# A causal-attention and two-MLP kernel on one Trainium2 core: a new order for the start of the attention, scores issued in two steps, and nine chunks of the third matrix prepared early

## The chip, the core and the metric

The kernel runs on one NeuronCore of a Trainium2 chip. Its engines take their instructions in order and independently of each other: TensorE (PE in the profile; its weight loads are PEld), VectorE (DVE), ScalarE (ACT), GpSimd (POOL), and SyncE (SP), which here only issues DMAs. The metric is the device time of one execution in microseconds (us).

## What is computed

```python
def _attn_ref(q, k, v):                       # each 2 x 12 x 448 x 64
    scores = np.matmul(q, k.transpose(0, 1, 3, 2)) / np.sqrt(64)
    scores = np.where(np.triu(np.ones((448, 448), bool), k=1), -1e9, scores)
    attn = np.exp(scores - np.max(scores, axis=-1, keepdims=True))
    attn = attn / (np.sum(attn, axis=-1, keepdims=True) + 1e-09)
    return np.matmul(attn, v)

def _moe_ref(x, w_in, w_out):                 # x: 896 x 768, w_in: 768 x 2048, w_out: 2048 x 768
    h = x @ w_in
    return (h * np.clip(h + 3.0, 0.0, 6.0) / 6.0) @ w_out

def _moe2_ref(x, w_in, w_out, a, b):          # the same sizes
    h = x @ w_in
    P = a[0] + a[1] * h + a[2] * h**2 + a[3] * h**3
    Q = 1.0 + np.abs(b[0]) * np.abs(h) + np.abs(b[1]) * h**2
    return (P / (Q + 1e-06)) @ w_out
```

The attention's result, with the heads side by side, is the `x` of the first MLP, and its result is that of the second. Weights come as float64.

## The kernel before

The 24 attention matrices (2 batches, 12 heads) are worked as 12 **pairs** n0 to n11: a pair is two heads of one batch (n = 2 hp + batch). In a pair the 448 rows of the scores are 7 blocks r of 64 rows, block r being 64(r+1) columns wide (causal). For each pair:

- **scores** (L458): 32 recorded matmuls on quarters of the array (64x64), all seven blocks at once, into four PSUM banks;
- **max** (L472, DVE), **exp** with its row sum (L479, ACT), both block by block; then for two groups of blocks, (6, 5, 0) and (4, 3, 2, 1): **bias** (L491, adds 1e-9 to the sums, POOL), **reciprocal** (L495, DVE) and **norm** (L501 on ACT, L503 on DVE and POOL);
- **transpose** (L511, two groups of 14 matmuls, array in two row halves, 64x128), and four **moves** (L346 on DVE, L344 on ACT) of the transposed blocks `et` out of PSUM;
- **apply** (L533, 36 recorded matmuls with V, array in two column halves, 128x64);
- **x hi** and **x rest** (L541 and L545): the result is split into a rounded part and a remainder, both fp32r.

The loads of q and k (`qk_load`, L414) and of V (`v_load`, seven DMAs per head pair) are issued on SP, but for two of the first pair's.

The four weight matrices (numbered 0 to 3) are cut in 128x128 tiles and stored three to a **chunk**: chunks 0 to 31 are matrix 0, 32 to 63 matrix 1, and from 64 on tiles of matrices 2 and 3 alternate. A chunk is loaded as 64-bit numbers (raw, five buffers), its top bits are taken on ACT (**top**, L662), joined on DVE (**join**, L667), rounded to fp32r (**w hi**, copied on ACT, POOL for some of the first four chunks) and its remainder taken (**w rest**, L685, DVE; POOL allowed for the first four). Some chunks of the last phase are prepared **early**, during matrices 0 and 1, written to DRAM (`kept`) and fetched back later: `early` holds the chunks c from `first` (64) up to the sixteenth from the end with c % 3 < 2. A **product** (L755) is one weight tile against both batches: six matmuls of 448 columns (hi-hi, hi-lo, lo-hi for each batch). There are 384 products, 2304 such matmuls. Products of matrix 0 may start as soon as a prepared chunk and the x of the first pairs are there; a few stand among the last pairs' attention.

What stands where is decided before the launch by a planner (class `Program`): it lists every step with the engines it may run on, an estimated cost, a time `at` and a table `DUE` of offsets per kind of step, places the steps on engines one by one, and then writes each engine's program in the planned order. At run time each engine goes through its own list in order and waits where its inputs are late.

At the start POOL fills `ident` and `mask`, and PE runs `WARM` matmuls of `ident` with itself that nobody reads (L398).

Of the kernel before, what the change touches and what calls it, by code (L numbers as in the profile page):

```python
# [20 lines left out]
CP = 64  # L21
NCH = 7
KC = 3
NA = 3
WARM = 10
SKEW = 64
LINE = 256
EARLY = 2, 3
LATE = 16
LAG = 3  # L30
MASKED = -8.0e9
# [9 lines left out]
class Program:  # L41
# [14 lines left out]
    BANKS = 8  # L56

    TILING = {"scores": "quarters", "transpose": "rows", "apply": "columns"}
    DRAIN = 0.16
    STAY = 11.93  # L60
    LOOK = {"pe": 0.302, "dve": 0.091, "act": 0.080, "pool": 0.000, "dma": 0.000}
    UNTIL = 90.0
# [5 lines left out]
    def add(self, kind, at, engines, fn, *args, reads=(), writes=(), new=()):  # L68

        self.ops.append((kind, at, engines, fn, args, tuple(reads), tuple(writes), tuple(new)))
# [150 lines left out]
def c_mm(n, passes):  # L223
# [4 lines left out]
DUE = {  # L228
    "load": 44.71,
    "keep": 0.00,  # L230
    "fetch": -20.00,
    "load v": -368.72,
    "norm": -159.02,
    "scores": 151.68,
    "max": -187.04,
    "exp": -138.64,
    "bias": -218.27,
    "reciprocal": -106.79,
    "transpose": -387.45,
    "move": 102.72,  # L240
    "apply": -96.69,
    "x hi": -163.28,
    "x rest": -28.48,
    "constants": 141.71,
    "w load": 418.94,
    "top": 318.26,
    "join": 411.50,
    "w hi": -217.67,
    "w rest": 106.68,
    "product": 0.00,  # L250
    "relu": -145.17,
    "gate": -250.64,
    "g hi": -349.62,
    "g rest": 161.82,
    "y hi": 20.80,
# [17 lines left out]
PAIR = 5.5  # L273
SHIFT = {0: -215.51, 1: -135.50, 2: -51.43, 10: 34.54, 11: 54.71}

# [19 lines left out]
def tile_attention_moe_moe2(  # L295
# [13 lines left out]
    B, D, H, S = qT.shape  # L309
# [4 lines left out]
    chunks = plan(KM, KF)  # L314
# [84 lines left out]

    add("constants", -50, {"pool": 1.5}, a_masks, writes=["masks"])  # L400
    for x in range(VB):
        add("constants", -49, {"pool": 0.4}, a_empty, x, writes=[("empty", x)])
    add(
        "constants", -49, {"pe": 0.4 * WARM}, a_warm, reads=["masks"], writes=["warm"],
        new=[("o", "warm")],
    )

    def qk_load(e, which, hp, batches):

        if (which, hp) not in tiles:  # L410
            tiles[which, hp] = at.tile([P, B, S], F32, tag=which, name=f"{which}{hp}", bufs=rings[which])
        src = (qT if which == "qr" else kT).rearrange("b d h s -> d b h s")
        for j in range(2):
            e.dma_start(tiles[which, hp][halves[j], batches], src[:, batches, 2 * hp + j])  # L414
# [10 lines left out]
    STRAIGHT, SWAPPED = (6, 5, 0), (4, 3, 2, 1)  # L425
    SCORES = 0, 2, 6, 4, 5, 1, 3
    BANKS = ((6, 0), (4, 2), (5,), (3, 1))
    GROUPS = [
# [15 lines left out]

    def a_scores(e, n, banks):
        q, k = (tiles[which, n // B][:, n % B] for which in ("qr", "kr"))
        for b, held in zip(banks, BANKS):
            col = 0
            for r in held:
                tiles["sc", n, r] = bank[b][:, col:col + (r + 1) * CP]  # L450
                col += (r + 1) * CP
        for r in SCORES:
            w = (r + 1) * CP
# [94 lines left out]

    order = 6, 0, 5, 4, 2, 3, 1
    for n in range(len(pairs)):  # L550
        t, last = PAIR * n + SHIFT.get(n, 0.0), n == len(pairs) - 1
        b, hp = pairs[n]
        for which in ("kr", "qr"):

            group, whole = (which, "all", hp), hp > 0
            if whole and b:
                continue
            add(
                "load", t, {"act" if n == 0 and which == "qr" else "dma": 1.26}, qk_load, which, hp,
                slice(0, B) if whole else slice(b, b + 1),  # L560
                writes=[(which, x) for x in range(n, n + (B if whole else 1))] + [group] * (b == 0),
                new=[(which, group)] if b == 0 else (),
            )
        if b == 0:
# [3 lines left out]
            )  # L568
        sc = [("sc", n, held) for held in BANKS]
        add(  # L570
            "scores", t, {"pe": 1.42}, a_scores, n, reads=[(w, *x) for w in ("kr", "qr") for x in ((n,), ("all", hp))],
            writes=sc + ["scored"] * last, new=[("s", key) for key in sc],
        )
        for late, r in enumerate(order):
            w, first, mine = (r + 1) * CP, late == 0, next(held for held in BANKS if r in held)
            add(
# [8 lines left out]
                writes=[("e", n, r), ("st", n, r)],  # L585
            )
        for part, held in enumerate((STRAIGHT, SWAPPED)):
            add(
                "bias", t + 2 * part, {"pool": 0.2}, a_bias, n, part,
                reads=[("st", n, r) for r in held] + [("stat", n)], writes=[("r", n, part)],  # L590
# [56 lines left out]

    add("constants", -55, {"pool": 0.7}, a_tops, writes=["tops"])

# [49 lines left out]
    def add_chunk(i, t, early=()):  # L699
# [12 lines left out]
        x = [("x", hp, b) for hp in range(KM) for b in range(B)] if early and i == early[0] else []  # L712
        act, dve = ({**e, "pool": c} if i < 4 else e for e, c in ((act, 0.5), (dve, 1.05)))
        add(
# [193 lines left out]
    first = next(c for c, what in enumerate(chunks) if what[0][0] == 2)  # L908
    early = [c for c in range(first, len(chunks) - LATE) if c % EARLY[1] < EARLY[0]]
    whole = first * KC * c_mm(S, 3 * B)  # L910
# [83 lines left out]
```

## Time and profile before

| | us |
|---|---|
| median of 3 runs (the other two 542.49 and 721.15) | 542.8 |
| the profiled execution, its own time | 541.71 |
| the profiled execution, span from first to last instruction | 539.9 |

| engine | busy us | share of the span |
|---|---|---|
| PE | 527.1 | 98% |
| DVE | 360.9 | 67% |
| ACT | 341.2 | 63% |
| POOL | 49.3 | 9% |

The mean granted TensorE clock is 0.994 of full speed (2.4 GHz); the DMA engines moved 164 GB/s on average. POOL works only in the first seventh of the span, where the attention is; after that PE runs products to the end. Matmul records overlap each other, so that a busy PE is not yet a PE at its peak: what it does in a stretch is better read from the starts of its groups of matmuls.

### The profile page before, as it was taken

What the parts mean: (1) busy time and instruction counts of PE and PEld (TensorE: products, weight loads), DVE (VectorE), ACT (ScalarE), POOL (GpSimd) and SP (SyncE); (2) the same over time, 40 slices, a digit from 0 to 9 for tenths busy, and PEclk for the clock granted to TensorE, in tenths of its full rate; (3) what the DMA queues carried; (4) which work ended last, traced back from release to release, by engine and by line L of the source; (5) the groups of instructions that cost most, each with busy time, mean ns of one, the idle gap of its engine ahead of it and who ended that gap; (6) DMA issues with size and microseconds to landing.
All of it is one profiled execution on the core that took longest, in us unless ns stands there. A gap on an engine that the chain in (4) does not pass through costs nothing.

```text
span 539.9 us, 9598 instructions
## 1 busy us (share of the span) xinstructions
PE 527.1 (98%) x3476; PEld 484.7 (90%) x3476; DVE 360.9 (67%) x801; ACT 341.2 (63%) x733; POOL 49.3 (9%) x116
## 2 busy tenths in 40 slices
PE   5899999999999999999999999999999999999997
PEld 5678879999999999999999999899999999999996
DVE  4699976677777765455443289988888888843310
ACT  4799966677777755555543299767776677645210
POOL 4598530000000000000000000000000000000000
PEclk9799999999999999999999999999999999999999
DMA  6886262487877777767774233432443244246000
GB/s 168 230 250 179 60 205 89 136 276 231 276 230 250 238 266 245 261 225 243 243 259 162 87 91 115 127 109 87 122 128 102 87 120 124 79 126 216 29 35 34
DMA packets 41583, 88.28 MB, mean 164 GB/s; under 512 B 4672, under 2 KB 16960, under 8 KB 41536
## 3 DMA queue, kind: packets, MB, share of 16 engines
q1 hardware_dynamic: 41376, 87.45, 51.7%
q8 instruction: 27, 0.44, 0.3%
q10 hardware_dynamic: 160, 0.23, 0.1%
q14 instruction: 20, 0.16, 0.1%
HBM read 72.32 MB, written 15.34 MB: 162 GB/s over the span
## 4 chain that ended last, share of the span: by engine, by line
PE 78%; DVE 6%; ACT 1%; DMA 1%; issue 1%; ACTq 0%
PE bank L755 77%; DVE p L804 1%; DVE qy L828 1%; DVE p L807 1%; DMA w<-kept 1%; DVE p L832 1%; PE bank L533 1%; DVE p L830 1%; DVE qy L820 1%; DVE rl L814 1%; DVE w L685 0%; ACT p L800 0%; ACT qy L794 0%; PE bank L511 0%; ACT top L662 0%
## 5 line engine op out<-in xcount | busy, mean ns | idle before, releaser
L685 DVE TENSOR_TENSOR w<-full,w 128x384 fp32r<-128x384 f32 x92 | 51.3, 557 | 111.4 <-ACT w L344 111.4
L755 PE MATMUL bank<-yh,w 128*128 128x448 f32 x384 | 112.7, 363 | 0.0
L662 ACT ACTIVATE top<-raw 128x384 f16<-128x384 bf16 x128 | 80.4, 639 | 49.3 <-DVE full L667 39.4
L344 ACT ACTIVATE w<-full 128x384 fp32r<-128x384 f32 x93 | 48.7, 524 | 80.6 <-PE bank L755 80.6
L755 PE MATMUL bank<-rh,w 128*128 128x448 f32 x384 | 97.2, 362 | 0.3 <-DMA w<-kept 0.3
L755 PE MATMUL bank<-xh,w 128*128 128x448 f32 x384 | 93.3, 363 | 0.0
L755 PE MATMUL bank<-ph,w 128*128 128x448 f32 x384 | 92.3, 361 | 0.0
L755 PEld LDWEIGHTS bank<-rh,w 128*128 128x128 f32 x384 | 71.8, 188 | 5.9 <-ACT qy L823 0.6
L755 PEld LDWEIGHTS bank<-yh,w 128*128 128x128 f32 x384 | 72.1, 188 | 5.3 <-DVE p L807 0.6
L755 PEld LDWEIGHTS bank<-ph,w 128*128 128x128 f32 x384 | 72.0, 187 | 4.9
L755 PEld LDWEIGHTS bank<-xh,w 128*128 128x128 f32 x384 | 71.6, 187 | 5.1
L667 DVE SCALAR_TENSOR_TENSOR full<-raw,top 128x384 uint32<-128x384 uint32 x128 | 68.9, 554 | 1.2 <-issue 0.3
L755 PE MATMUL bank<-yl,w 128*128 128x448 f32 x192 | 69.2, 361 | 0.0
L755 PE MATMUL bank<-rl,w 128*128 128x448 f32 x192 | 54.5, 362 | 0.0
L755 PE MATMUL bank<-xl,w 128*128 128x448 f32 x192 | 54.2, 363 | 0.0
L755 PE MATMUL bank<-pl,w 128*128 128x448 f32 x192 | 54.2, 363 | 0.0
L479 ACT ACTIVATE e<-e,stat 128x448 f32<-128x448 f32 (+6 forms) x84 | 41.6, 499 | 10.0 <-DVE stat L472 8.8
L755 PEld LDWEIGHTS bank<-yl,w 128*128 128x128 f32 x192 | 35.9, 187 | 2.5
L755 PEld LDWEIGHTS bank<-xl,w 128*128 128x128 f32 x192 | 36.0, 188 | 2.4
L755 PEld LDWEIGHTS bank<-pl,w 128*128 128x128 f32 x192 | 36.0, 188 | 2.3
L472 DVE CUSTOM_DVE_ANT_0 e<-bank,mask 128x256 f32<-128x256 f32 (+6 forms) x84 | 30.6, 414 | 11.2 <-PE bank L458 11.1
L755 PEld LDWEIGHTS bank<-rl,w 128*128 128x128 f32 x192 | 36.0, 187 | 2.3
(58 smaller groups left out, 633.6 us busy)
## 6 DMA issues: line engine op xcount, KB each, us to landing
raw<-in_w SPq DMA_DIRECT2D x128, 383.8 KB, 3.8
kept<-ws SPq DMA_DIRECT2D x32, 384.0 KB, 4.4
w<-kept SPq DMA_DIRECT2D x32, 384.0 KB, 3.4
out_T<-o SPq DMA_DIRECT2D x12, 224.0 KB, 2.1
kr<-in_kT SPq DMA_DIRECT2D x10, 224.0 KB, 3.8
qr<-in_qT SPq DMA_DIRECT2D x10, 224.0 KB, 4.5
v<-in_v SPq DMA_DIRECT2D x12, 128.0 KB, 3.9
v<-in_v SPq DMA_DIRECT2D x12, 96.0 KB, 3.7
```

The source lines that it names most:

```text
L344: e.activation(out, in_, AF.Copy)
L472: e.tensor_tensor_reduce(e_tile(n, r), tiles.pop(("sc", n, r)), over, -0.125, 3.0e38, ALU.add, ALU.min, tiles["stat", n][:, 0, at_:at_ + 1],)
L479: e.activation(t, t, AF.Exp, bias=stat[:, 0, at_:at_ + 1], scale=-1.0, accum_out=stat[:, 1, at_:at_ + 1],)
L533: e.matmul(o[halves[j], r * CP:(r + count) * CP], vt[:, c, halves[j]], et[slot][:, x * CP:(x + count) * CP], start=g == 0 and m == 0, stop ...
L662: e.activation(out, raw[i].bitcast(BF16)[:, :, :, 2], AF.Copy)
L667: e.scalar_tensor_tensor(full[i].bitcast(U32), bits, 13, top.pop(i), ALU.logical_shift_right, ALU.bitwise_or)
L685: e.tensor_tensor(split[i][:, 1], full.pop(i), split[i][:, 0], ALU.subtract)
L755: e.matmul(sums[which, m, b], split[i][:, w, j, :], x, start=k == 0 and n == 0, stop=last and n == 2,)
L804: e.tensor_tensor(p, p, h, ALU.mult)
L807: e.scalar_tensor_tensor(p, p, cneg[:, 1:2], h, ALU.add, ALU.mult)
L814: e.tensor_tensor(gs[3, b, m][1], p, gs[3, b, m][0], ALU.subtract)
L820: e.tensor_tensor(q, q, y, ALU.mult)
```

## The change

- `WARM`, the number of unread matmuls, goes from 10 to 6, and POOL fills `ident` and `mask` first and the two `top` buffers last instead of first.
- The first two pairs' q and k loads are single steps per half: one half of each is issued on SP and the other may be issued on ACT. The table's new numbers put the loads of the second head pair ahead of the first V.
- Scores are two steps of two banks, blocks (5, 4, 2) and (6, 3, 0, 1), instead of one of four; max and exp run over the blocks in the order 5, 6, 0, 4, 2, 3, 1 (as the table lets them), no longer 6, 0, 5, 4, 2, 3, 1.
- For pairs n0, n10 and n11 the bias is done on ACT or DVE, and no longer on POOL.
- The remainder of a weight chunk is never taken on POOL.
- The first nine chunks of the last phase (64 to 72) are all early: 35 early chunks, 32 before.
- `DUE`, `SHIFT`, `STAY`, `LOOK` have other numbers, and `HURRY` moves the later steps of the first and last pairs.

```diff
-WARM = 10
+WARM = 6
+WHOLE = 9
...
-    add("constants", -50, {"pool": 1.5}, a_masks, writes=["masks"])
+    add("constants", -60, {"pool": 1.5}, a_masks, writes=["masks"])
...
-    SCORES = 0, 2, 6, 4, 5, 1, 3
-    BANKS = ((6, 0), (4, 2), (5,), (3, 1))
+    BANKS = (((5,), (4, 2)), ((6, 0), (3, 1)))
+    SCORES = (5, 4, 2), (6, 3, 0, 1)
...
-    order = 6, 0, 5, 4, 2, 3, 1
+    order = 5, 6, 0, 4, 2, 3, 1
...
+            for parts in ((0,), (1,)) if n == 0 else ((0, 1),):
+                add(
+                    "load", t, {"act" if parts == (1,) else "dma": 0.63 * len(parts)}, qk_load, which, hp,
...
+        for step in range(2):
+            sc = [("sc", n, held) for held in BANKS[step]]
+            add(
+                "scores", t + step, {"pe": 0.71}, a_scores, n, step,
...
-                "bias", t + 2 * part, {"pool": 0.2}, a_bias, n, part,
+                "bias", t + 2 * part, {"pool": 0.2} if 0 < n < 10 else {"act": 0.2, "dve": 0.1}, a_bias, n, part,
...
-    add("constants", -55, {"pool": 0.7}, a_tops, writes=["tops"])
+    add("constants", -40, {"pool": 0.7}, a_tops, writes=["tops"])
...
-        act, dve = ({**e, "pool": c} if i < 4 else e for e, c in ((act, 0.5), (dve, 1.05)))
+        if i < 4:
+            act = {**act, "pool": 0.5}
...
-    early = [c for c in range(first, len(chunks) - LATE) if c % EARLY[1] < EARLY[0]]
+    early = [
+        c for c in range(first, len(chunks) - LATE) if c < first + WHOLE or c % EARLY[1] < EARLY[0]
+    ]
```

What this moves on the engines is seen at three places. The first is SP's list from its start; `kr0`, `qr0` are the first head pair (n0 and n1), `kr1`, `qr1` the second (n2 and n3), `v0` the first V. Before:

```order
L414 DMA kr0_107<-in_kT 64x448 x4
L414 DMA qr0_112<-in_qT 64x448 x2
L419 DMA v0_99<-in_v 64x4x128
L420 DMA v0_99<-in_v 64x3x128
L419 DMA v0_99<-in_v 64x4x128
L420 DMA v0_99<-in_v 64x3x128
L422 DMA v0_99<-in_v 64x2x128 x3
L414 DMA kr1_183<-in_kT 64x2x448 x2
L414 DMA qr1_191<-in_qT 64x2x448 x2
```

In the change (ACT's list begins with one `kr0` and one `qr0` load, where it had two of `qr0`):

```order
L417 DMA kr0_107<-in_kT 64x448
L417 DMA qr0_121<-in_qT 64x448
L417 DMA kr0_107<-in_kT 64x448 x2
L417 DMA qr0_121<-in_qT 64x448 x2
L417 DMA kr1_140<-in_kT 64x2x448 x2
L417 DMA qr1_151<-in_qT 64x2x448 x2
L422 DMA v0_99<-in_v 64x4x128
```

The four loads for n2 and n3 went ahead of the seven of V.

The second place is ACT's list in the middle of the attention; `e` rows are exps, `et` rows moves, `xh` rows x hi. Before, from the first exp of n6:

```order
L479 ACTIVATE e00_91,stat6_703<-e00_91,stat6_703 128x448
L479 ACTIVATE e00_91,stat6_703<-e00_91,stat6_703 128x64
L479 ACTIVATE e20_93,stat6_703<-e20_93,stat6_703 128x384
L479 ACTIVATE e10_92,stat6_703<-e10_92,stat6_703 128x320
L344 ACTIVATE xh1_84<-bank1_74 128x448
L479 ACTIVATE e10_92,stat6_703<-e10_92,stat6_703 128x192
L479 ACTIVATE e30_94,stat6_703<-e30_94,stat6_703 128x256
L479 ACTIVATE e30_94,stat6_703<-e30_94,stat6_703 128x128
L344 ACTIVATE et5_0_1_795<-bank7_80 128x448
```

In the change, from the first exp of n4:

```order
L482 ACTIVATE e20_93,stat4_461<-e20_93,stat4_461 128x384
L347 ACTIVATE et3_0_0_551<-bank4_77 128x448
L482 ACTIVATE e00_91,stat4_461<-e00_91,stat4_461 128x448
L482 ACTIVATE e00_91,stat4_461<-e00_91,stat4_461 128x64
L482 ACTIVATE e10_92,stat4_461<-e10_92,stat4_461 128x320
L347 ACTIVATE xh0_82<-bank1_74 128x448
L482 ACTIVATE e10_92,stat4_461<-e10_92,stat4_461 128x192
L482 ACTIVATE e30_94,stat4_461<-e30_94,stat4_461 128x256
L482 ACTIVATE e30_94,stat4_461<-e30_94,stat4_461 128x128
L347 ACTIVATE et3_1_1_611<-bank2_75 128x448
```

A pair's stretch of ACT's list now holds two moves in place of one; over all pairs ACT has 26 of the 48 moves, 13 before.

The third place is PE's list where pair n4 gets its scores. Before, one block of 16 matmuls (32 records in the trace):

```order
L458 MATMUL bank1_74<-kr2_284,qr2_295 64x64 x2
L458 MATMUL bank2_75<-kr2_284,qr2_295 64x64
L458 MATMUL bank2_75<-kr2_284,qr2_295 64x128
L458 MATMUL bank2_75<-kr2_284,qr2_295 64x64
L458 MATMUL bank2_75<-kr2_284,qr2_295 64x128
L458 MATMUL bank1_74<-kr2_284,qr2_295 64x448 x2
L458 MATMUL bank2_75<-kr2_284,qr2_295 64x320 x2
L458 MATMUL bank7_80<-kr2_284,qr2_295 64x384 x2
L458 MATMUL bank6_79<-kr2_284,qr2_295 64x128 x2
L458 MATMUL bank6_79<-kr2_284,qr2_295 64x256 x2
```

In the change, the first half of the same scores with the transposes on either side of it:

```order
L514 MATMUL bank1_74<-ident_89,e11_96 128x64
L461 MATMUL bank4_77<-kr2_238,qr2_265 64x384 x2
L461 MATMUL bank5_78<-kr2_238,qr2_265 64x320 x2
L461 MATMUL bank5_78<-kr2_238,qr2_265 64x64
L461 MATMUL bank5_78<-kr2_238,qr2_265 64x128
L461 MATMUL bank5_78<-kr2_238,qr2_265 64x64
L461 MATMUL bank5_78<-kr2_238,qr2_265 64x128
L514 MATMUL bank7_80<-ident_89,e20_93 128x64
```

The second half stands further down, behind the apply of n1 and ahead of the next transposes. Up to the last pair's apply PE's list has 56 groups (runs of scores, of transposes, of applies or of products), 46 before; and 42 matmuls of 448 columns (seven products) stand ahead of that apply, 18 (three products) before.

## Rows read from the trace of the kernel before

**Rows 1.** Stretches: length; busy us of PE, PEld, DVE, ACT, POOL; granted clock; DMA share, GB/s.
```profile
6.12:21.76 15.64, 10.65 (x171) 8.17 (x171) 10.55 (x52) 11.35 (x43) 4.05 (x11) 0.78 0.77 199
35.75:64.37 28.62, 28.62 (x580) 23.60 (x576) 28.28 (x120) 27.62 (x99) 22.04 (x54) 1.00 0.58 150
8.04:78.72 70.68, 63.81 (x1135) 51.78 (x1128) 63.82 (x252) 63.08 (x212) 44.87 (x101) 0.95 0.67 183
15.00:19.00 4.00, 3.62 (x36) 2.60 (x36) 0.93 (x6) 1.96 (x9) 0.66 (x2) 0.50 0.66 178
```
**Rows 2.** Chain that ended last, in order of time: start us, us, what.
```profile
77.78 230.62 PE bank L755 x1152
...
350.45 185.90 PE bank L755 x927
```
**Rows 3.** Timeline of PE, first 24 us: start us, us, group xcount [idle before].
```profile
2.05 4.13 PE L398 MATMUL bank<-ident 128*128 128x128 f32 x20 [2.05 <-POOL ident masks.py:199]
6.12 3.33 PE L458 MATMUL bank<-kr,qr 64*64 64x64 f32 x64
...
14.70 0.47 PE L458 MATMUL bank<-kr,qr 64*64 64x64 f32 x2 [2.78 <-DMA qr<-in_qT]
15.55 3.27 PE L458 MATMUL bank<-kr,qr 64*64 64x64 f32 x30 [0.38 <-DMA qr<-in_qT]
...
21.76 1.99 PE L533 MATMUL bank<-et,v 128*64 128x128 f32 x36
```
**Rows 4.** Timeline of PE later in the attention and at its end.
```profile
35.75 0.65 PE L511 MATMUL bank<-ident,e 64*128 64x64 f32 x14
...
55.41 1.76 PE L458 MATMUL bank<-kr,qr 64*64 64x64 f32 x32
57.11 0.64 PE L511 MATMUL bank<-ident,e 64*128 64x64 f32 x14
57.68 1.99 PE L533 MATMUL bank<-et,v 128*64 128x128 f32 x36
...
60.18 1.76 PE L458 MATMUL bank<-kr,qr 64*64 64x64 f32 x32
...
77.71 0.68 PE L755 MATMUL bank<-xh,w 128*128 128x448 f32 x2
```
**Rows 5.** DMA issues on the SP and ACT lists (timeline: start us, us, xcount).
```profile
0.72 2.49 SPq L414 DMA_DIRECT2D kr<-in_kT  x4
0.75 1.46 ACTq L414 DMA_DIRECT2D qr<-in_qT  x2
...
10.46 1.26 SPq L414 DMA_DIRECT2D qr<-in_qT  x2
```
**Rows 6.** DMA issues near 1.35 and 11 us: KB each, us from issue to landing.
```profile
qr<-in_qT ACTq DMA_DIRECT2D x1, 112.0 KB, 3.7
...
qr<-in_qT SPq DMA_DIRECT2D x2, 224.0 KB, 4.3
```
**Rows 7.** First exp on ACT (timeline), and all exps of the page.
```profile
8.04 0.67 ACT L479 ACTIVATE e<-e,stat 128x448 f32<-128x448 f32 x1 [6.04 <-DVE stat L472]
...
L479 ACT ACTIVATE e<-e,stat 128x448 f32<-128x448 f32 (+6 forms) x84 | 41.6, 499 | 10.0 <-DVE stat L472 8.8 <-DVE stat L495 0.8
```
**Rows 8.** Groups by shape, first 80 us: moves, remainders on POOL: busy, mean ns.
```profile
L346 DVE COPY et<-bank 128x448 f32<-128x448 f32 x35 | 21.1, 609 | 0.2 <-PE bank L511 0.2
...
L344 ACT ACTIVATE et<-bank 128x448 f32<-128x448 f32 x13 | 6.7, 530 | 0.3 <-PE bank L511 0.3
...
L685 POOL TENSOR_TENSOR w<-full,w 128x384 fp32r<-128x384 f32 x4 | 4.4, 1100 | 0.3
```
**Rows 9.** Timeline of POOL: the norms of one group of three, one of four.
```profile
18.34 1.49 POOL L503 TENSOR_SCALAR e<-e,stat 128x448 f32<-128x448 f32 x3 [3.72 <-DVE stat L495]
...
21.65 1.73 POOL L503 TENSOR_SCALAR e<-e,stat 128x320 f32<-128x320 f32 x4 [1.52 <-DVE stat L495]
```

More of the change, by code (lines that the diff above doesn't have):

```diff
@@ L59 @@
     DRAIN = 0.16
-    STAY = 11.93
-    LOOK = {"pe": 0.302, "dve": 0.091, "act": 0.080, "pool": 0.000, "dma": 0.000}
+    STAY = 13.14
+    LOOK = {"pe": 0.086, "dve": 0.083, "act": 0.049, "pool": 0.064, "dma": 0.000}
     UNTIL = 90.0
@@ L228 @@
 DUE = {
-    "load": 44.71,
+    "load": -129.37,
     "keep": 0.00,
     "fetch": -20.00,
[L232 to L249, printed above, removed]
+    "load v": 83.26,
+    "norm": -184.88,
+    "scores": 113.76,
+    "max": 232.08,
+    "exp": 280.78,
+    "bias": 209.88,
+    "reciprocal": -166.73,
+    "transpose": -481.36,
+    "move": 288.15,
+    "apply": -515.99,
+    "x hi": 234.09,
+    "x rest": 470.59,
+    "constants": 166.20,
+    "w load": 15.29,
+    "top": 271.52,
+    "join": 538.78,
+    "w hi": 373.92,
+    "w rest": 100.25,
     "product": 0.00,
[L251 to L254, printed above, removed]
+    "relu": -472.26,
+    "gate": -35.40,
+    "g hi": -141.53,
+    "g rest": 443.84,
     "y hi": 20.80,
@@ L273 @@
 PAIR = 5.5
-SHIFT = {0: -215.51, 1: -135.50, 2: -51.43, 10: 34.54, 11: 54.71}
+SHIFT = {0: -54.00, 1: -36.74, 2: -35.18, 3: -15.52, 10: 33.70, 11: 140.79}
+HURRY = {0: -193.16, 1: -356.33, 2: -518.72, 3: -470.02, 10: -219.85, 11: -513.15}
 def plan(KM, KF):
@@ L403, in tile_attention_moe_moe2, with qk_load @@
     add(
-        "constants", -49, {"pe": 0.4 * WARM}, a_warm, reads=["masks"], writes=["warm"],
+        "constants", -59, {"pe": 0.45 * WARM}, a_warm, reads=["masks"], writes=["warm"],
         new=[("o", "warm")],
     )
-    def qk_load(e, which, hp, batches):
+    def qk_load(e, which, hp, batches, parts):
         if (which, hp) not in tiles:
@@ L412, in qk_load @@
         src = (qT if which == "qr" else kT).rearrange("b d h s -> d b h s")
-        for j in range(2):
+        for j in parts:
             e.dma_start(tiles[which, hp][halves[j], batches], src[:, batches, 2 * hp + j])
@@ L443, in slots, with a_scores @@
         return (0, 1) if r in STRAIGHT else (1, 0)
-    def a_scores(e, n, banks):
+    def a_scores(e, n, step, banks):
         q, k = (tiles[which, n // B][:, n % B] for which in ("qr", "kr"))
-        for b, held in zip(banks, BANKS):
+        for b, held in zip(banks, BANKS[step]):
             col = 0
@@ L451, in a_scores @@
                 col += (r + 1) * CP
-        for r in SCORES:
+        for r in SCORES[step]:
             w = (r + 1) * CP
@@ L557, in tile_attention_moe_moe2 @@
                 continue
[L558 to L563, printed above, removed]
+            for parts in ((0,), (1,)) if n == 0 else ((0, 1),):
+                add(
+                    "load", t, {"act" if parts == (1,) else "dma": 0.63 * len(parts)}, qk_load, which, hp,
+                    slice(0, B) if whole else slice(b, b + 1), parts,
+                    writes=[(which, x, j) for x in range(n, n + (B if whole else 1)) for j in parts],
+                    new=[(which, group)] if b == 0 and 0 in parts else (),
+                )
         if b == 0:
@@ L568, in tile_attention_moe_moe2 @@
             )
[L569 to L573, printed above, removed]
+        for step in range(2):
+            sc = [("sc", n, held) for held in BANKS[step]]
+            add(
+                "scores", t + step, {"pe": 0.71}, a_scores, n, step,
+                reads=[(w, *x) for w in ("kr", "qr") for x in ((n, 0), (n, 1), ("all", hp))],
+                writes=sc + ["scored"] * last, new=[("s", key) for key in sc],
+            )
         for late, r in enumerate(order):
-            w, first, mine = (r + 1) * CP, late == 0, next(held for held in BANKS if r in held)
+            w, first, mine = (r + 1) * CP, late == 0, next(h for step in BANKS for h in step if r in h)
             add(
@@ L586, in tile_attention_moe_moe2 @@
             )
+        t += HURRY.get(n, 0.0)
         for part, held in enumerate((STRAIGHT, SWAPPED)):
             add(
-                "bias", t + 2 * part, {"pool": 0.2}, a_bias, n, part,
+                "bias", t + 2 * part, {"pool": 0.2} if 0 < n < 10 else {"act": 0.2, "dve": 0.1}, a_bias, n, part,
                 reads=[("st", n, r) for r in held] + [("stat", n)], writes=[("r", n, part)],
```

## The prediction

> **What bounds the kernel now.** I read the chain that ended last first. It runs on PE's products without a break of note from 77.78 us to the end: 1152 matmuls of 448 columns in 230.62 us [rows 2], 0.2002 each, so that all 2304 are worth 461.2 us, which the change neither removes nor speeds up. The last ones end at 350.45 + 185.90 = 536.35 [rows 2]; the 3.55 us from there to the span's 539.9 (last moves and stores) stand in the same order before and after. What is left to win lies ahead of 77.71.
>
> There the timeline of PE tells two stages apart. From 35.75 to 64.37 its groups follow each other without a gap, PE 28.62 of 28.62, DVE 28.28, ACT 27.62 [rows 1]: a pair takes 60.18 - 55.41 = 4.77 us [rows 4], of which scores are 1.70 (to the next start), transposes 0.57 to 0.58 twice and the apply 1.92. Twelve pairs are 57.2 us. With the three products that stand ahead of 77.71 (some 4.2 us) and the 6.12 us before the first score, 10.2 us of the first 77.71 are lost. Most of them are early: by 35.75 PE had done six pairs' scores, eight groups of transposes and three applies, 6 x 1.70 + 8 x 0.58 + 3 x 1.92 = 20.6 us of work, in 29.6 us after the first score. The reader sees why in the first rows: n2's scores wait 2.78 us for q at 14.70, again at 15.55, and then run at half the granted clock [rows 1, 3].
>
> **The first score.** The scores at 6.12 begin as the ten unread matmuls end (2.05 + 4.13) [rows 3]. Six of these take 2.5 us and end before 4.6 even if `ident` came no sooner. Then the loads decide: two of the four halves are issued on ACT as before, the second near 1.35, and that one landed 3.7 us later [rows 6], at 5.05. With 0.15 for the hand-over the scores start at 5.2, 0.9 earlier. n1's four loads keep their places in SP's list.
>
> **The first exp.** It came 8.04 - 6.12 = 1.92 after the scores' start [rows 3, 7]. Blocks 0, 2 and 6 (704 columns) stood first and block 6 opened; now it is block 5, 384 columns and alone. A pair's 1792 columns take 1.70, so this is 0.30 less, and a narrower max saves about 0.06: first exp at 5.2 + 1.56 = 6.76, or 1.28 earlier.
>
> **The loads of n2 and n3.** An SP issue takes 0.62 [rows 5]. The last q load of this pair stood behind seven of V, at about 11.1, and landed 4.3 later [rows 5, 6], at 15.4, when PE went on (15.55). Now six are ahead of these four, the last issue is near 6.4 and the landing near 10.7. V then follows from 7.0 to 11.5; even with the 4.3 of the larger loads it is there at 15.8, more likely nearer 14.
>
> **To the first apply.** n0's exps are 41.6 / 12 = 3.47 us [rows 7] and end near 10.3. Sums, bias (now on DVE, a shape not seen there; its POOL bound is a quarter us, nothing the other), reciprocal and norms of the second group take some 2 us, of which POOL's norms are 1.5 to 1.7 [rows 9]: transposes at 12.3. Half of n2's scores stand ahead of n0's transposes in PE's list and are through by 11.65, so they hold up nothing. Two moves of 0.6 on each engine, on DVE behind about 1 us of other work, put the apply at about 15.0; it was at 21.76 [rows 3].
>
> **From there to the third apply's end**, before 35.75 - 21.76 = 13.99 us for 12.06 of PE work (three applies, two pairs' scores, five transposes). By the new lists the work between these two points is the same amount. I laid the next pairs out row by row with the durations above. PE has no wait until n3's first transposes: n2's last exp ends near 20.9, POOL's four norms of n2 (1.73) end near 23.8, then n3's bias, reciprocal and three norms (1.49 [rows 9]) near 25.85, and PE is there at 24.5. So 12.06 + 1.35 gives 28.4 against 35.75. But n5's scores and one transpose group, 2.27 us, are then still to do: 7.35 - 2.27 = 5.1 us ahead.
>
> **The rest of the attention.** Two things cost. PE's list has 56 groups to the last apply and not 46; one fewer of the first 14, so 11 more behind the third apply. What a group costs beyond its matmuls is seen where two pairs' scores run on: 64 records in 3.33 us, 32 in 1.76 [rows 3, 4], so the second half adds 1.57, where a pair's scores between transposes take 1.70 to the next start: 0.12 to 0.13 each way. Eleven are 1.3 us. The page TensorEngine Tiling (Array Packing) of the Trainium skill, section Tiling Modes, says that changing the tiling mode drains TensorE, and the scores, transposes and applies are three modes; the trace agrees, with 0.12 us a change. Without that rule the gain would be 5.6 and not 4.3.
>
> The other is ACT. It takes 13 moves from DVE (13 to 26 of 48) [rows 8], about 0.42 each without the overlap of the records, so 5.5 us, less one w hi and some norms (1.7). It was busy 63.08 of the 70.68 us from its first exp to its last x hi [rows 1]; now about 66.9. DVE loses 13 moves of 0.55 and gains four w rests of some 0.5 that POOL did in 1.1 each [rows 8], so it is no longer the full engine. A pair's ACT work is then 3.47 + 3 x 0.42 = 4.7, just under PE's 4.77: I take no wait for it, and from its idle time the rival below.
>
> In the last 13.3 us before 77.71 PE lost about 1.1 (three applies, four groups of transposes and three products are 12.3). Now four more products stand there, which fill waits and are paid back later; what they fill I put at 0.5. The three more early chunks change ACT's and DVE's work between 80 and 300 us, where PE never waits, and take some from the start of the last phase. PE lost at most 536.35 - 77.71 - 2286 x 0.2002 = 1.0 us in all products, so that is the most this edit can bring; I take nothing. If the cover is gone, a late chunk costs one wait of PE of about its landing, 4 us.
>
> Sum: 5.1 - 1.3 + 0.5 = 4.3 us ahead once both have done the same products. The profiled execution took 541.71 (span 539.9 and 1.8 around it), so 537.4; the median of the runs, 542.8, lies 1.1 above it, so **538.5**.
>
> **Rivals.** *No wait at all after the first apply*: without the 1.35 at n3 and the 0.6 that I leave at the end, 6.3 us are won: 536.5. For it speaks that PE ran 28 us without a gap before; against it that POOL's norms come late in the new order of exps, and that ACT would have to be idle less than 3 us of 70, where it was 7.6 [rows 1].
>
> *The clock falls as before.* From 15 to 19 the granted clock was 0.50, the lower level (1.2 GHz), after PE had done one group of transposes (0.65 us) between 9.44 and 14.70; n2's scores took 3.27 for 30 records and not 1.76 for 32 [rows 1, 3, 4]. In the change PE has about 2.9 us of work between 8.5 and 15.0. If the clock is low when the first apply comes, that apply lasts 3.8, and with what is behind it 1.8 are lost until it is granted again: 540.3.
>
> *POOL's wait comes back with each pair* (the other side). The wait of 1.35 at n3 rests on a chain exp, bias, reciprocal, three norms that every pair from n1 to n9 has. If six more pairs pay it, 8.1 are lost: 546.6, slower. It decides from three more pairs on. Against it: before, POOL did the same seven norms for each pair and was busy 22.04 of the 28.62 us in which PE never waited [rows 1], and it now has 6 us less.
>
> *The loads were not what held n2*: then its scores come at 15 as before, and only the start (1.3) is won, minus 1.3 of groups: no change, 542.8. The wait on q in rows 3 speaks against it.
>
> **How the numbers follow.** My forecast 0.50, with 537.0 to 540.0; no wait 0.22; the clock 0.17; POOL or loads 0.08; anything that costs or gives over 2% (10.9 us, about what a measurement of this kernel can tell from no change) 0.03, since the 10.2 us lost and the 0.9 at the start would all have to go, or two or three chunks to come late. From 534.8 (no wait, the changes of mode at nothing, 535.2, and the first apply a little sooner) to 541.8 (the clock, and V 0.8 later or one more wait for POOL) some 0.82 is held. Faster by over 2%: 0.02; slower: 0.02.
>
> **What will show it.** Right: first score near 5.2 and first exp near 6.8; n2's first scores near 10.8 without a wait at 15; the first apply near 15 and the third's end near 28; the last apply's end near 78 with 42 product matmuls ahead of it; no POOL remainder; products at 0.200 us. Wrong: a granted clock of 0.5 behind 12 us; PE waiting for POOL's norms in every pair; ACT idle over 7 us between its first exp and last x hi; a wait of PE behind 80 us for a chunk.

## The result and the profile after

The change takes 537.52 us (median) where the kernel before, beside it on the same chip, takes 542.64: a ratio of 0.9905 [0.9883, 0.9928] (95% interval), faster by about 1%. Run twice more beside the experiments below it gave 0.9912 [0.9897, 0.9928] and 0.992 [0.9905, 0.9934]. Each median counts one execution that took far longer (721.15 us before, 1062.74 after) and tells nothing of the change. The profiled execution took 537.43 with a span of 535.7 (before 541.71 and 539.9). The forecast was 538.5, most likely 537.0 to 540.0; the time lies in that range, 1.0 below its middle.

The profiled executions differ by 4.3 us and the medians by 5.1: the profile of before was taken of an execution 0.9 below its median. What follows accounts for the profiled ones.

Steps of the chain that ended last, of the kernel after (start us, us, what):

```profile
1.36 3.37 DMA qr<-in_qT
...
4.87 6.36 PE bank L461 x43
...
22.44 1.73 POOL e L506 x4
...
24.25 0.25 POOL stat L494
...
24.86 1.21 POOL e L506 x2
...
26.12 0.65 PE bank L514 x14
...
79.52 452.64 PE bank L763 x2262
```

From 79.52 the products run to 532.16 in one piece, 2262 in 452.64 us, 0.2001 each. Before, the chain left PE between its two long pieces [rows 2]: 350.45 + 185.90 = 536.35, less 77.78 and 2286 x 0.2001 = 457.4, leaves 1.1 us lost there. So of 536.35 - 532.16 = 4.2 us won, 1.1 are won in the products and the other 3.1 in the attention: 77.71 [rows 4] plus the 24 further matmuls that now stand ahead of the last apply (4.8) less its end at 79.45 is 3.06.

The timeline of PE after, its start (start us, us, group xcount, idle before and what ended it):

```profile
1.34 2.93 PE L401 MATMUL bank<-ident 128*128 128x128 f32 x12 [1.34 <-POOL ident masks.py:199]
4.87 7.39 PE L461 MATMUL bank<-kr,qr 64*64 64x384 f32 x80 [0.60 <-DMA qr<-in_qT]
12.96 0.65 PE L514 MATMUL bank<-ident,e 64*128 64x64 f32 x14 [0.70 <-POOL e L506]
14.26 0.65 PE L514 MATMUL bank<-ident,e 64*128 64x64 f32 x14 [0.64 <-POOL e L506]
...
15.85 1.99 PE L536 MATMUL bank<-et,v 128*64 128x128 f32 x36
...
26.12 0.65 PE L514 MATMUL bank<-ident,e 64*128 64x64 f32 x14 [0.21 <-POOL e L506]
26.70 1.99 PE L536 MATMUL bank<-et,v 128*64 128x128 f32 x36
28.62 1.15 PE L461 MATMUL bank<-kr,qr 64*64 64x384 f32 x16
29.70 0.65 PE L514 MATMUL bank<-ident,e 64*128 64x64 f32 x14
30.28 1.08 PE L461 MATMUL bank<-kr,qr 64*64 64x448 f32 x16
31.30 0.65 PE L514 MATMUL bank<-ident,e 64*128 64x64 f32 x14
```

The wait of 2.78 us for q and the half pace behind it [rows 3] are gone: the scores of n0, n1 and half of n2's run in one piece of 80 records from 4.87. But that piece takes 7.39 us, where 64 records took 3.33 before [rows 3]; the experiments come back to it. The third apply ends at 28.62 (35.75 before [rows 4]), and from there PE has no gap to the end.

The page of after, its busy times, and two stretches (length; busy us of PE, PEld, DVE, ACT, POOL; granted clock; DMA share, GB/s):

```profile
PE 528.7 (99%) x3468; PEld 484.9 (91%) x3468; DVE 360.0 (67%) x800; ACT 340.5 (64%) x743; POOL 44.9 (8%) x107
```
```profile
28.00:64.37 36.37, 36.37 (x660) 28.72 (x655) 31.54 (x139) 35.98 (x124) 25.55 (x60) 1.00 0.67 179
6.90:79.40 72.50, 70.95 (x1182) 56.97 (x1174) 61.24 (x253) 66.46 (x221) 40.52 (x92) 1.00 0.69 188
```

ACT is now busy 66.46 us (63.08 before [rows 1]) and nearly full where PE is full; DVE has room.

### The profile page after: what moved, and what is told of

Its sections match the earlier page's. It is cut to its first block, busy times and chain, and to the rows that moved or that the text cites. A ratio compares the mean times of both kernels' runs of the same rounds, so it can differ in the third digit from the quotient of the medians.

```text
span 535.7 us, 9569 instructions
## 1 busy us (share of the span) xinstructions
PE 528.7 (99%) x3468; PEld 484.9 (91%) x3468; DVE 360.0 (67%) x800; ACT 340.5 (64%) x743; POOL 44.9 (8%) x107
## 4 chain that ended last, share of the span: by engine, by line
PE 97%; DVE 1%; POOL 1%; DMA 1%; issue 0%; SPq 0%; ACT 0%; POOLq 0%
PE bank L763 86%; PE bank L461 4%; PE bank L536 4%; PE bank L514 2%; POOL e L506 1%; DMA qr<-in_qT 1%; DVE e L475 0%; DVE et L349 0%; SPq L417 0%; ACT o L347 0%; DVE stat L498 0%; DVE w L692 0%; DVE e L506 0%; POOL stat L494 0%; DVE stat L494 0%
## 5 line engine op out<-in xcount | busy, mean ns | idle before, releaser
L347 ACT ACTIVATE w<-full 128x384 fp32r<-128x384 f32 x89 | 46.6, 523 | 66.7 <-PE bank L763 66.7
L482 ACT ACTIVATE e<-e,stat 128x384 f32<-128x384 f32 (+6 forms) x84 | 41.7, 501 | 6.0 <-DVE stat L475 5.8
L475 DVE CUSTOM_DVE_ANT_0 e<-bank,mask 128x448 f32<-128x448 f32 (+6 forms) x84 | 31.8, 413 | 11.4 <-PE bank L461 8.8
```

What stands on the lines that cost most here:

```text
L347: e.activation(out, in_, AF.Copy)
L475: e.tensor_tensor_reduce(e_tile(n, r), tiles.pop(("sc", n, r)), over, -0.125, 3.0e38, ALU.add, ALU.min, tiles["stat", n][:, 0, at_:at_ + 1],)
L482: e.activation(t, t, AF.Exp, bias=stat[:, 0, at_:at_ + 1], scale=-1.0, accum_out=stat[:, 1, at_:at_ + 1],)
```

## Experiments

Ratios are to the kernel before, run beside each on the same chip, with 95% intervals.

### The load order: taken back, and alone

The theory is that the order of loads brings the attention's part of the gain. Taken back in the change (n2's and n3's q and k behind the first V again, nothing else):

```python
late = [s for s in steps if s[0][0] == "load" and s[0][4][1] == 1]   # head pair 1
steps = [s for s in steps if s not in late]
v = next(x for x, s in enumerate(steps) if s[0][0] == "load v")
steps[v + 1:v + 1] = late
```

> The change with the four q and k loads of n2 and n3 back behind the seven of the first V on SP; all else as in the change. Theory (moving these loads is most of the early gain): their last issue is near 11 and lands near 15.4, n2's first scores start there, and n0's transposes, which stand behind them on PE, near 16.5 (12.96 in the change), the first apply comes near 19.5 (15.85) and the median is 3 to 4 above the change, about 541. Rival (the loads were not what held the start): within 0.5 of the change.

Measured 542.58, ratio 1.0011 [1.0002, 1.0019]: nothing of the gain is left, although the other parts of the change are in place. PE's timeline of this run:

```profile
5.27 5.54 PE L466 MATMUL bank<-kr,qr 64*64 64x384 f32 x64 [1.00 <-DMA qr<-in_qT]
14.70 3.02 PE L466 MATMUL bank<-kr,qr 64*64 64x384 f32 x16 [3.89 <-DMA qr<-in_qT]
...
20.62 1.99 PE L541 MATMUL bank<-et,v 128*64 128x128 f32 x36
```

n2's scores wait 3.89 us for q up to the very time of before, 14.70, and half a pair's scores then take 3.02 us (1.08 to 1.15 in the change). The load order is necessary. Is it sufficient? In the kernel before, only these four loads go ahead of the first V:

```diff
-        for (_, _, _, fn, args, _, _, _), e, banks in self.order():
+        steps = self.order()
+        early = [s for s in steps if s[0][0] == "load" and s[0][4][1] == 1]
+        steps = [s for s in steps if s not in early]
+        v = next(x for x, s in enumerate(steps) if s[0][0] == "load v")
+        steps[v:v] = early
+        for (_, _, _, fn, args, _, _, _), e, banks in steps:
```

> The kernel before with one edit: the four q and k loads of n2 and n3 ahead of the first V on SP. Theory: n2's scores follow n0's first transposes without the wait (near 11.9, not 14.70 and 15.55), the first apply comes near 17.5 (21.76), and 2 to 4 us are won, about 539. Rival (the first stage is bound by ACT, DVE and POOL whatever the loads do): under 0.5 won, 542.

Measured 542.37, ratio 1.0007 [0.9996, 1.0019]: no change. PE's timeline says why:

```profile
12.49 1.76 PE L463 MATMUL bank<-kr,qr 64*64 64x64 f32 x32
...
17.71 1.99 PE L538 MATMUL bank<-et,v 128*64 128x128 f32 x36
...
24.73 0.44 PE L463 MATMUL bank<-kr,qr 64*64 64x64 f32 x2 [4.44 <-DMA qr<-in_qT]
25.74 3.27 PE L463 MATMUL bank<-kr,qr 64*64 64x64 f32 x30 [0.57 <-DMA qr<-in_qT]
```

n2's scores start at 12.49 without a wait and the first apply comes at 17.71, 4 us sooner than before [rows 3]. Then n4's scores wait 4.44 us for their q, whose loads stand behind the seven of the second V as well. The same stall stands one head pair further on, with the same half pace (30 records in 3.27, the granted clock 0.50 from 24.7 to 29), and the third apply ends at 37.50, later than before. In the change these loads stand ahead of the second V as well, which the prediction did not look at: it laid out SP's list of the change only up to the first V. So the next run moves both:

```diff
         steps[v:v] = early
+        vs = [s for s in steps if s[0][0] == "load v" and s[0][4][0] == 1]
+        steps = [s for s in steps if s not in vs]
+        last = max(x for x, s in enumerate(steps) if s[0][0] == "load" and s[0][4][1] == 2)
+        steps[last + 1:last + 1] = vs
```

> The kernel before with two moves on SP's list alone: q and k of n2 and n3 ahead of the first V, and q and k of n4 and n5 ahead of the second V; scores stay one step of four banks, nothing else is changed. Theory (the load order is sufficient once both pairs of loads go ahead of V; the run with the first move alone lost its gain in a wait of 4.4 + 0.6 us for the q of n4): no wait of PE for a q over 1 us behind 10 us, first apply near 17.7, the third apply's end at 30 to 32 (35.75 before), 3.5 to 5.5 us won, 537.2 to 539.2, ratio 0.990 to 0.9935. Rival A (the stall goes on to the next thing late, V of n2 and n3 or the loads of n6 and n7): third apply's end near 32, but a new wait of 2 us or more for a load between 25 and 45 us, under 1 us won, ratio 0.998 to 1.000. Rival B (without scores in two steps the lead is lost in waits for PSUM banks, DVE being busy 28.3 of 28.6 us): third apply's end near 31, the lead half gone by 64 us in waits for POOL's or DVE's work, ratio 0.994 to 0.997.

Measured 538.71, ratio 0.9939 [0.9925, 0.9952], 3.5 us: the theory's time, at the low end of its gain (ratio and third apply's end lie just outside its bounds). PE's timeline:

```profile
17.64 1.99 PE L542 MATMUL bank<-et,v 128*64 128x128 f32 x36
...
25.87 1.99 PE L542 MATMUL bank<-et,v 128*64 128x128 f32 x36 [1.03 <-ACT et L353]
...
30.77 1.99 PE L542 MATMUL bank<-et,v 128*64 128x128 f32 x36
32.69 0.65 PE L520 MATMUL bank<-ident,e 64*128 64x64 f32 x14
...
37.45 0.65 PE L520 MATMUL bank<-ident,e 64*128 64x64 f32 x14
```

No q is waited for, the third apply ends at 32.69 (3.1 us sooner than before), and the pairs behind it run at 37.45 - 32.69 = 4.76, as before. Of this lead (how far PE is ahead of the kernel before at the same work) 2.9 us are there at the last apply's end (74.82 against 77.71 [rows 4]): neither DVE nor POOL takes it back, so rival B falls too. The other 0.4 of the profiled execution's 3.3 came in the products. Two moves on one queue's list are thus the larger part of the whole change.

### The nine early chunks: taken back, and alone

In the change, `WHOLE` 9 to 0:

> The change with the 32 early chunks of before in place of 35 (chunks 65, 68 and 71 prepared in their turn); the attention's lists are the same. Theory (the three more early chunks took away 1.1 us that PE lost in products at 336 to 341, 350 and 394 before): PE loses about 1.1 again at such places, and the median is about 538.6. Rival (those waits came from the early stage's order and went with it): no losses, 537.5.

Measured 539.10, ratio 0.9945 [0.993, 0.9961], where the two variants with nine chunks and more unread products (below) that shared its chip took 537.59 and 538.07. The largest of its waits among the products, in PE's timeline:

```profile
327.85 0.37 PE L763 MATMUL bank<-yl,w 128*128 128x448 f32 x1
329.39 0.67 PE L763 MATMUL bank<-yh,w 128*128 128x448 f32 x2 [1.17 <-DVE w L692]
```

From start to start this is 1.34 us more than a matmul's 0.20; with shorter ones the products lose about 2.0. Without the edit the changed order, which has its attention done sooner, loses more there than the kernel before did (1.1). And alone, in the kernel before:

```diff
-    early = [c for c in range(first, len(chunks) - LATE) if c % EARLY[1] < EARLY[0]]
+    early = [
+        c for c in range(first, len(chunks) - LATE) if c < first + 9 or c % EARLY[1] < EARLY[0]
+    ]
```

> The kernel before with one edit of the change alone: the first nine chunks of the last phase are all early (35 early chunks, not 32). Theory (the nine chunks are a part of the gain by themselves): the products behind the attention run without the 1.0 to 1.2 us of waits that they have before, so 541.4 to 541.6 against 542.6, a ratio of 0.9975 to 0.998, and products at 0.2001 us each from their first to their last; the attention ends at 77.7 +- 0.3. Rival (the nine chunks pay only together with the new order, which leaves other work at the start of the last phase): ratio 0.999 to 1.001, with waits of PE of 0.4 us or more still among the products.

Measured 541.25, ratio 0.9982 [0.9973, 0.999]: 0.9 us by itself. The end of its chain:

```profile
77.95 457.53 PE bank L755 x2286
```

2286 products in 457.53 us, 0.2001 each, with no loss. Together with the 3.5 of the load order this is 4.4 us, as much as the change itself won beside these two on one chip (542.17 to 537.75). These two parts were not run together without others; where they were (four parts, below), 3.0 came.

### The start: how many unread products

The slow piece of scores at 4.87 was the one row that the prediction did not have at all. Theory: six unread matmuls leave TensorE at its lower clock when the scores come, though the granted clock of that stretch reads 1.00. `WARM` 6 to 10 in the change:

> The change with ten unread products at the start, as before, in place of six; every list is otherwise the same. In the change the first scores ran at half the pace of before (a 448-column record lasted 1.0 us, before 0.54) though the granted clock in the trace reads 1.00 there. Theory (the array was still at its lower clock since six unread products, 2.9 us, end before it rises): with ten the unread products last from 1.34 to about 5.5, the 448-column records fall to about 0.55, the scores of n0 and n1 are through by about 8.8 (11.2 in the change), the first apply starts near 15.0 (15.85) and the median falls by 0.5 to 1.0, to about 536.6. Rival (the slow records were waiting for q and k): the records stay near 1.0, the first score comes 0.6 later, and the time is 537.5 to 538.1.

Measured 538.07, ratio 0.9921 [0.9905, 0.9937]: the same as the change, and not the 536.6 of the theory. PE's timeline:

```profile
5.75 3.33 PE L461 MATMUL bank<-kr,qr 64*64 64x384 f32 x64
10.84 2.32 PE L461 MATMUL bank<-kr,qr 64*64 64x384 f32 x16 [1.76 <-DMA qr<-in_qT]
13.09 1.76 PE L514 MATMUL bank<-ident,e 64*128 64x64 f32 x28
14.78 1.54 PE L461 MATMUL bank<-kr,qr 64*64 64x448 f32 x16
16.25 1.99 PE L536 MATMUL bank<-et,v 128*64 128x128 f32 x36
```

The first 64 records now take 3.33. But n2's q lands no sooner, so PE waits 1.76 us for it, and behind this wait the granted clock falls (a stretch of the same run, columns as above):

```profile
13.00:15.00 2.00, 2.00 (x34) 1.79 (x36) 0.83 (x2) 0.86 (x4) 0.11 (x1) 0.50 0.76 214
```

In that stretch, at 0.50 (1.2 GHz), 28 transposes take 1.76 us (0.65 for 14 in the change); half a pair's scores behind them take 1.54, not 1.08, and the first apply comes 0.4 later than in the change. What was saved at 5 us is paid at 13. Eight unread matmuls lie between:

> The change with eight unread products. They end near 5.0, where the loads land (4.73). Theory: if eight are enough for the clock, the first score stays near 5.0, scores run at the full pace, and the median is about 536.3; if not, scores are slow as with six and the time stays near 537.5. Rival (waiting for q and k): as with six, 537.5.

Measured 537.59, ratio 0.992 [0.9903, 0.9938]. The 64 records take 4.40, q is waited for 0.79 us, the clock record shows no fall, and the first apply comes at 14.68, 1.2 us before the change's. The last apply ends 0.8 sooner (its products start at 78.68 and not at 79.52), which the times of whole executions cannot tell from nothing. Nor do the profiles: in two more executions of the change itself, with six, the first apply came at 15.29 and 15.27 and the products behind the last apply at 78.91 and 79.12, so that part of these differences is one of executions and not of kernels.

### Scores in two steps

In the change, with the second half of each pair's scores put directly behind the first on PE's list, for six pairs (n4, n5, n6, n8, n10 and n11), where no step comes to stand before one that it needs:

```python
x, y = pe.index(first), pe.index(second)          # a pair's two score steps
moved = pe[:x + 1] + [second] + [n for n in pe[x + 1:] if n != second]
if y > x + 1 and run({**lists, "pe": moved}):      # no step before one that it needs
    pe = moved
```

> The change with the second half of a pair's scores pulled up directly behind the first on PE wherever the banks allow it, so that eight fewer groups stand ahead of the last apply (whole scores of four later pairs among them); the other engines' lists are the same. Theory (PE is what bounds the attention behind 28 us, and a split pair's scores cost 2.10 us where a whole one costs 1.70 to the next start): 1.5 to 2.5 us less, about 535.5. Rival (ACT, busy 35.98 of the 36.37 us from 28.00 to 64.37, bounds as much as PE): PE's shorter list turns into waits, the time stays within 0.5 of 537.5, and PE shows waits on ACT's and DVE's results.

Measured 540.43, ratio 0.9967 [0.9955, 0.998]: slower than the change, by more than theory or rival had. Its stretch from 28 to 64.37 and what PE waited for over the span (us in total, times, longest):

```profile
28.00:64.37 36.37, 34.61 (x658) 27.83 (x654) 29.50 (x134) 33.73 (x116) 25.41 (x60) 1.00 0.66 171
```
```profile
PE bank L588 <- POOL e L580: 2.4, 5, 0.7
...
PE bank L535 <- ACT et L421: 0.8, 2, 0.6
```

The saving of a joined pair is real (1.73 us to the next start at 29.70, where a split one took 2.10), but PE is now idle 1.76 us of the stretch and the third apply ends at 29.70. The waits for POOL's norms are 2.4 us (1.6 in the change), those for moves on ACT are new. My theory that PE alone is the limit there falls. Is it ACT, which was nearly full? The same kernel with five moves of n4 to n8 given from ACT to DVE:

```diff
+SHIFTED = (4, 1, 1), (6, 1, 1), (7, 0, 1), (7, 1, 1), (8, 1, 1)
...
+        steps = [
+            (op, "dve" if op[0] == "move" and op[4] in SHIFTED else e, banks) for op, e, banks in steps
+        ]
```

> The kernel with joined score halves (it took 540.4, with waits of PE on ACT's moves and POOL's norms) and five moves of n4 to n8 taken from ACT back to DVE, which was busy 29.5 of the 36.37 us from 28.00 to 64.37 there. Theory (ACT, busy all but 0.4 of 36.4 us in the change, is the second bound, and joining only brought it out): with 2.1 us less on ACT the last apply ends near 78.5 (82.5 with the joined halves alone) and the time is near 536. Rival (joining lost because a pair's second half has to wait for its banks and holds up the transposes behind it): the time stays near 540.

Measured 541.46, ratio 0.9994 [0.9981, 1.0007]: slower again, with ACT at 30.79 and PE at 34.30 of the same stretch. What the scores wait for in this run:

```profile
PE bank L539 <- DVE et L427: 0.8, 2, 0.4
PE bank L539 <- DVE stat L553: 0.4, 1, 0.4
```

So it is not ACT's load alone: with less of it the waits go over to the engine that took the moves. My reading of these rows, which no run tests by itself: the second half's scores need two further PSUM banks, which come free only with moves and maxima; put early, they stand at the head of PE's list and hold up the transposes behind them. In this order of the other engines' lists, split scores let PE fill that time, for 0.4 us a pair. That they pay at all is not shown: the kernel before keeps its scores whole, its banks are free in time by its own lists, and with the loads moved alone it wins 3.5 us.

### Four parts together, without the rest

The kernel before with both load moves, `ident` and the masks first, eight unread matmuls and the nine chunks; scores whole, moves and biases as before:

```diff
+        tops = [s for s in steps if s[0][3].__name__ == "a_tops"]
+        steps = [s for s in steps if s not in tops]
+        first = next(x for x, s in enumerate(steps) if s[0][0] == "bias")
+        steps[first:first] = tops
...
-        for _ in range(WARM):
+        for _ in range(8):
```

> The kernel before with four parts of the change, but not with scores in two steps, nor its new moves and table: q and k of n2 to n5 ahead of the V that they stood behind, ident and the masks first on POOL, eight unread products, nine chunks early. Theory (these four parts are the whole gain, and whole scores save about 0.2 us a pair): first score near 5.0, the attention's end 4 to 6 us sooner than before, products without loss: 535.5 to 537.5, ratio 0.987 to 0.9905, as fast as the change or up to 2 us faster. Rival (scores in two steps are needed to keep the lead): 538.5 to 540.5, ratio 0.9925 to 0.996, with waits of PE behind 30 us for POOL, DVE or ACT that the change doesn't have.

Measured 539.15, ratio 0.9936 [0.9921, 0.9951], its runs spread from 537.4 to 539.5: by the median in the rival's range, and no better than the load moves by themselves. But the rival's waits behind 30 us are not there, beyond the one of 1.16 at 70.53 that the kernel before has too (1.05); what there is stands at 25.86. Its first score comes at 5.06, 1.6 sooner than with the load moves alone (6.62). Then (PE, a stretch with columns as above, and ACT of the profiled execution, 539.51 us; the second fence is ACT of the run with the load moves alone):

```profile
25.86 2.91 PE L546 MATMUL bank<-et,v 128*64 128x128 f32 x36 [1.90 <-ACT et L357]
28.70 2.43 PE L471 MATMUL bank<-kr,qr 64*64 64x64 f32 x32
...
25.86:28.70 2.84, 2.84 (x36) 2.36 (x36) 1.73 (x7) 2.50 (x9) 1.83 (x5) 0.65 1.05 270
...
24.79 0.64 ACT L675 ACTIVATE top<-raw 128x384 f16<-128x384 bf16 x1 [1.85 <-DMA raw<-in_w]
25.29 0.95 ACT L357 ACTIVATE et<-bank 128x448 f32<-128x448 f32 x2
```
```profile
24.80 0.63 ACT L671 ACTIVATE top<-raw 128x384 f16<-128x384 bf16 x1 [0.99 <-DMA raw<-in_w]
25.30 0.95 ACT L353 ACTIVATE et<-bank 128x448 f32<-128x448 f32 x2
```

In both kernels ACT stands at the first weight chunk's top until that chunk lands, at 24.8, and two moves of n2 are behind it on ACT's list. n1's apply needs none of their results (its own moves are on DVE), but the bank that one of them frees. All that the earlier start brought ends there; it only makes the wait longer, and behind the wait of 1.90 the granted clock of 25.86 to 28.70 reads 0.65, the apply takes 2.91, not 1.99, and the scores behind it 2.43, not 1.76: 1.6 us. The spread of the six runs goes with this: the two of 537.37 and 537.67 had a mean granted clock of 1.00 and 0.999, the four of 538.98 to 539.51 one of 0.993 to 0.997. The change itself, once more on this chip:

> The change itself once more, beside the three parts of it on the same chip: ratio 0.990 to 0.992, the first score at 4.9, the third apply's end at 28.6, the last apply's end at 79.4. If its ratio lies under that of the four parts together, scores in two steps and the new moves are worth something by themselves.

0.992 [0.9905, 0.9934], 1.4 us under the four parts, with intervals that overlap. Whether the rest of the change (split scores, moves, biases, table) is worth that 1.4 us is not settled; in the two executions that kept the clock the four parts were as fast as the change. What an earlier start lacks in the old lists is, by these rows, another place for that one top: in the change it stands behind n6's exps on ACT's list and runs at 41.0. Moving it alone was not tried. The other run of the change as a control had

> The change itself once more, beside the runs below on their chip: about 0.9905 of the kernel before (537 where that is 542).

and gave 537.07, 0.9912 [0.9897, 0.9928]. No run beats the change measurably.

## Why the prediction was right, and where its steps were not

**The sum.** The profiled execution was put at 537.4 and took 537.43; that this is so close is luck, as the terms below show. The 1.0 by which 538.5 is too high is the 1.1 added because the median before lay that far above its profiled execution; after the change it lies 0.1 above.

**The bound.** Right: products at 0.2001 us each to the end, the gain ahead of 77.71, and most of that early, in n2's wait for q. Taking the load order back shows it: 1.0011.

**The loads.** The mechanism was right, and one place was missed. The working stopped at the first V; the loads of n4 and n5 ahead of the second V are as necessary in the old lists, as the run with the first move alone shows (4.44 us of waiting at 24.73). The rows laid out behind the first apply had these loads in time, as the change has, but not as something that the change had to move.

**First score**, predicted 5.2: 4.87. The load issued at 1.36 landed 3.37 us later, not 3.7.

**First exp**, predicted 6.76: 7.43, though the scores started sooner. The step that failed is the price of the scores: n0's first half at 1.70 a pair. 64 records that took 3.33 before [rows 3] ran at about half pace behind six unread matmuls (80 in 7.39). The prediction weighed the clock at 15 us and not at 5.

**First apply**, predicted 15.0: 15.85, from the late exp and two waits of 0.70 and 0.64 for POOL's norms. **Third apply's end**, predicted 28.4: 28.62. The chain exp, norms, bias, norms of n2 and n3 is the one named and ends at 26.12 (25.85 predicted); PE came later to it and so waited 0.21 and not 1.35. The lead there was 35.75 - 28.62 - 2.27 = 4.9, predicted 5.1: two misses that cancelled.

**The rest of the attention**, predicted 0.8 lost (1.3 for groups, 0.5 back): 4.9 - 3.06 = 1.8 were lost. The mis-sized term is the price of a group. I took 0.12 from scores that ran on behind scores; a pair's scores split between transposes measure (29.70 - 28.62) + (31.30 - 30.28) = 2.10 against 1.70 whole [rows 4], so 0.40. Five pairs are split behind 28.62, 2.0 us; one pair's joined halves took 0.3 more; two more groups of products at 0.2 are 0.4. Against these 2.7 PE got back the whole 1.1 that it had lost before 77.71, and not 0.5. That makes 1.6; of the 0.2 that are left, 0.1 is one pair of transpose groups that ran on as one before (1.02 us to the next start at 65.78) and now stand apart (0.58 each). The page TensorEngine Tiling (Array Packing) of the Trainium skill, section Tiling Modes, says that a change of mode drains TensorE; the trace agrees, with 0.40 for the two that a split pair adds, though no run here tells a drain from another cost of the switch.

**ACT.** Right in size (66.9 busy predicted, 66.46), and that it makes no wait: PE is full while ACT is 35.98 of 36.37. **POOL's wait with each pair** did not come: three waits, 1.6 us, all before 26.2.

**The products**, predicted 0 and at most 1.0: 1.1 were won, and alone the edit wins 0.9. I had named that most and taken nothing, because PE never waits between 80 and 300 us and a chunk was thought to be hidden in any case. What it buys lies at 327 to 394 us, where PE waited for a chunk's remainder on DVE or for a fetched chunk; in the changed order it is worth 1.0 to 1.5 us (539.10 against 537.59 and 538.07). Why those chunks were late in the first place was not tried. This miss and that of the groups have about the same size and opposite signs, and the forecast is as near as it is because of it: luck.

**The clock falls as before** (0.17): not in the change by its record, but the rival's mechanism came with ten unread matmuls and with the four parts together, behind waits of 1.8 to 1.9 us, and with the loads taken back, where the granted clock reads 0.53 from 13 to 15, at the end of the wait of 3.89; and the change ran its first scores at about half pace at 5 us instead.

## What to carry to other kernels

Read the issue list of the queue that feeds the start as far as the first stretch in which the bounding engine is full, and ask of each load which engine stops first if it is late: putting what is needed sooner ahead of what is needed later won 3.5 of 4.4 us here, and only when it was done for two rounds, since with one round the same stall came back in the next. A start that is made faster is worth nothing where a later landing sets the pace (n2's q at 10.8, the first weight chunk at 24.8), so name the next landing before pricing the gain. Where steps are split or interleaved on a full engine, price the change of shape in the place where it will stand, between the very neighbours it will have.

## What the runs showed of the hardware

Matmuls ran at about half pace while the granted clock read 1.00. The records of 64x448 between 4.8 and 10 us, by shape (busy us, mean ns), of the change and then of the run with ten unread matmuls:

```profile
L461 PE MATMUL bank<-kr,qr 64*64 64x448 f32 x6 | 2.9, 968 | 0.0
```
```profile
L461 PE MATMUL bank<-kr,qr 64*64 64x448 f32 x8 | 1.9, 544 | 0.0
```

The only edit between the two is four more unread matmuls. With eight the mean of this shape is 630 ns, and in the two further executions of the change 757 and 761. The page TensorE: Matmul & The Clock Gate of the Trainium skill says, in its section Part 1: The HAM clock gate, that the lower clock (1.2 GHz) is the default until activity releases it, and warns that the trace's clock events are not always to be trusted; both fit these two rows, but no record here shows the lower level before the first wait. A start is therefore better judged from the mean of one shape than from the granted clock.

A wait of 1.76 us at 10.84 (ten unread matmuls) and one of 1.90 at 25.86 (the four parts) were followed by a lower granted clock, and one of 1.81 at 10.96 in that last run was not; what decides between them is left open.
